# First inverse stage of a long convolution moved to two 64-row PE tiles, with a new order, engine choice and bank plan

## The chip, the cores and the metric

The kernel runs on one core of a Trainium2 chip. The metric is the device time of one execution in microseconds (us), lower is better. A core has five engines with queues of their own: TensorE (PE, matmuls into PSUM), VectorE (DVE), ScalarE (ACT), GpSimd (POOL) and SyncE (SP, which here issues nearly all DMAs). An engine works through its queue in order; semaphores make one engine wait for another.

## The reference, cut to what matters

Two layers, each a gated long convolution ("A") and an MLP ("B"), over 2048 tokens of 512 channels in bfloat16. Both layers use the same weights, and the convolution's inputs k and v do not depend on the layer, so its result y is needed only once.

```python
def _A_ref(q, k, v, shift_k, ssm_k, ssm_D):
    ...                                   # k_shift: causal 4-tap filter of k per channel
    kv = k_shift * v
    ...                                   # pad kv and ssm_k to 2*S, rfft2 of both
    y = irfft2(kv_f * kf_f)[:S]           # causal convolution of kv with ssm_k, per channel
    y = y + kv * ssm_D
    return q * y

def _B_ref(x, w1, b1, w2, b2):
    y = _layernorm(x)
    h = gelu(y @ w1 + b1)
    return h @ w2 + b2

x = A_q
x = x + _A_ref(_layernorm(x), A_k, A_v, A_shift_k, A_ssm_k, A_ssm_D)
x = x + _B_ref(_layernorm(x), B_w1, B_b1, B_w2, B_b2)
x = x + _A_ref(_layernorm(x), ...)        # the same y again
x = x + _B_ref(_layernorm(x), ...)
```

## The kernel before

**The convolution.** It is done by matmuls as a two-stage transform of 1024 points a half, the sequence being cut into two halves (tags end in _0 and _1). For the filter ("h") and for the product kv ("x") there is a first stage (`stage1`, L570, matmul L578: eight tiles of two PSUM banks, each of 16 matmuls) and a second (`stage2`, L583, matmul L590: eight tiles t of 16 matmuls). Every tile is then copied out of PSUM by ACT or DVE (`evac`, L477, with ACT at L480 and DVE at L481). The second stage reads a table of 16384 columns, R_S2. Its upper half is loaded by eight DMAs; its lower half (t below 4) is spread out on the chip from a compact table R_C of 1024 columns: eight operations, "spread" (L510 to L521), each multiply the compact table by a 0/1 mask of the partitions and write every eighth group of 16 columns. So the first second-stage tile with t below 4 needs all eight. They may go to ACT (L519) or DVE (L520). The filter is copied once more with its halves of the partitions exchanged, by DMAs called `swap` (L595).

Spectra are multiplied on DVE (L475, "products": for each of the eight tiles of x2_0 two of 128x1024, called g = 0 and g = 1). `inverse1` (L678, matmul L695) is the first inverse stage: eight tiles j of two banks. The tiles j = 0 to 3 read the products g = 0 of all eight x2_0 tiles, the tiles j = 4 to 7 the products g = 1. Its argument `split` chooses between two forms of the same sum: whole, 16 matmuls a tile with 128 rows of contraction and 128 columns; or split, 32 matmuls a tile, each with 64 rows of contraction and 64 columns, alternating between rows 0 to 63 (first bank) and rows 64 to 127 (second bank). The table R_U has zeros between the two halves of the rows, so both compute the same. Half 0 calls it whole (tag i1_0, L776), half 1 split (tag i1_1). `inverse2` (L705, matmul L717) is the second inverse stage: its matmuls read the results of all eight tiles of `inverse1`. Half 1 has the stages of its own (h2_1, p2, x1_1, x2_1, sum, i1_1, i2_1), which run while the MLP of half 0 does.

**The MLP.** Tokens go in blocks q0 to q12 of 128 to 512. For a block: statistics (bn_stats L831, L832), the reciprocal root on POOL (L836, L838), the normalisation on ACT or DVE (L856, L857), product with y and sum (L475), statistics again, normalisation, transposition (by PE for the first two token tiles, L908, else by DMA, L900), 11 tiles of the first matmul (m1, L920) with GELU on ACT (L925), and the second matmul (m2, L954) added on DVE (L958).

**The order.** The program is first written down as 1187 operations with a number each. Three literals then fix everything: SEQ is the order in which all operations are put on their engines' queues, ENGS names the engine (a, v, p) of each of the 233 operations that may go to more than one, BANKS gives the first PSUM bank of each of the 291 tiles. `arrange` (L214) applies them and adds the waits for PSUM banks; `sync` (L248) works out the semaphore waits. The numbers in `P.op(..., dur)` are the planner's costs; at run time they do nothing.

Of the kernel before, what the change touches and what calls it, by code (L numbers as in the profile page):

```python
# [36 lines left out]
class Prog:  # L37
# [62 lines left out]
    ENGS = (  # L100
            "pvavvvvvavpvpapapaaavaaaaavaavaavavvvppvvvaavvaaavaavvaaaaaaaaavaaaaavaaaavaaaaaaapppvaaaaaaaaaaaaaaaaaa"
            "avaaaaaaaaapvapvvavpvppaappvvpvaavpaappaappaappaappaappavppvappaappaappvappaapvaapvavvavvvvvapvvvvvppvaa"
            "avvvvaappavvapvavavpvvava")
    BANKS = (
# [294 lines left out]
def bass_interleave_layers__ssm_conv_h3__mixer_channel_mlp__prompt_kernel(  # L399
        nc, A_q, A_k, A_v, A_shift_k, A_ssm_k, A_ssm_D, B_x, B_w1, B_b1, B_w2, B_b2, out):  # L400
    P = Prog(nc)
# [101 lines left out]

    tload(t_s2, 18432, 0, R_C, 1024)
    load_h(0, R_1)
    load_t(A_k, 0, R_8, 2)
    load_t(A_v, 0, R_8 + 4096, 2)
    for i in range(8, 16):
        tload(t_s2, 18432, 2048 + i * 1024, R_S2 + i * 1024, 1024)
# [485 lines left out]
```

## Time and profile before

| what | value |
|---|---|
| time, median of 3 runs | 236.95 us (236.3 to 237.21) |
| span of the profiled execution, first to last instruction | 234.0 us |
| PE busy | 222.7 us, 95% of the span |
| DVE busy | 178.7 us, 76% |
| ACT busy | 164.5 us, 70% |
| POOL busy | 55.5 us, 24% |
| L695 whole (i1_0), 128 matmuls | 7.4 us busy |
| L695 split (i1_1), 256 matmuls | 5.0 us busy |
| granted TensorE clock | 1.000 |

The profiled execution's time is known by its span of 234.0 us; what lies around the span (launch and end) is the rest of an execution's time, 2.95 us by the median. In the rows quoted below, a row of the timeline gives start, duration, engine, line, operation, tiles and count, and in brackets the idle time before it; a row of the chain of waits gives start, duration and what the end of the program was waiting for then. A matmul's row ends when its last result lands, so a row is some 0.2 us longer than the time it keeps the next one back.

### The profile page before, as it was taken

The numbers are of one execution on the slowest core, as the hardware profiler recorded it, in microseconds if no ns is written. First come the engines' busy times: TensorE is split into PE (matmuls) and PEld (weight loads), VectorE is DVE, ScalarE is ACT, GpSimd is POOL, SyncE is SP. The second block draws the span as 40 slices with busy tenths as digits, with TensorE's granted clock in tenths as the row PEclk, the third lists the DMA queues.
The fourth block names the chain that finished last, engine by engine and source line by source line (L and its number), as shares of the span: only waits on it lengthen the run. The fifth ranks groups of instructions, "written<-read, shape, count | busy, mean of one in ns | idle before, by whom it ended". The sixth has DMA issues, their size and how long they took to land.

```text
span 234.0 us, 6498 instructions
## 1 busy us (share of the span) xinstructions
PE 222.7 (95%) x2743; PEld 147.1 (63%) x2765; DVE 178.7 (76%) x362; ACT 164.5 (70%) x262; POOL 55.5 (24%) x113
## 2 busy tenths in 40 slices
PE   7989887999999999999999999999999999999995
PEld 3878776967868596677966576644444444444454
DVE  0699998999999999999999988781777569410222
ACT  2789999989968688999879986488058216802710
POOL 2270132006403405639303331204011120200000
PEclk9999999999999999999999999999999999999999
DMA  6999489928994360033500313401300130170202
GB/s 185 381 386 305 147 229 274 324 65 150 144 211 126 70 158 3 1 48 72 155 4 3 90 24 68 134 3 22 69 0 3 28 62 0 23 115 0 90 0 92
DMA packets 40106, 24.93 MB, mean 107 GB/s; under 512 B 23591, under 2 KB 33677, under 8 KB 40077
## 3 DMA queue, kind: packets, MB, share of 16 engines
q1 hardware_dynamic: 39778, 24.36, 39.7%
q8 instruction: 22, 0.36, 0.7%
q10 hardware_dynamic: 298, 0.16, 0.4%
q14 instruction: 8, 0.06, 0.1%
HBM read 13.23 MB, written 2.10 MB: 66 GB/s over the span
## 4 chain that ended last, share of the span: by engine, by line
PE 58%; DVE 24%; ACT 10%; issue 2%; POOL 2%; DMA 2%; SPq 0%; DVEq 0%
PE ps L920 23%; PE ps L954 23%; DVE ar L475 13%; ACT ar L480 9%; PE ps L695 4%; DVE sm L831 3%; PE ps L590 2%; DMA ar<-in_A_ssm_k_dram 2%; DVE ar L672 2%; DVE ar L958 2%; DVE ar L641 2%; PE ps L717 1%; POOL sm L836 1%; PE ps L578 1%; PE ps L635 1%
## 5 line engine op out<-in xcount | busy, mean ns | idle before, releaser
L925 ACT ACTIVATE ar<-ps,sm 128x256 bf16<-128x256 f32 (+5 forms) x143 | 65.7, 523 | 33.2 <-PE ps L920 32.9
L920 PE MATMUL ps<-ar 128*128 128x256 bf16 (+5 forms) x569 | 81.9, 297 | 0.4 <-ACT ar L480 0.2
L480 ACT ACTIVATE ar<-ps 128x1024 bf16<-128x1024 f32 (+3 forms) x77 | 71.1, 998 | 11.0 <-PE ps L578 3.4
L954 PE MATMUL ps<-ar 128*128 128x512 bf16 (+1 forms) x323 | 75.9, 379 | 1.5 <-issue 0.6
L920 PEld LDWEIGHTS ps<-ar 128*128 128x128 bf16 (+1 forms) x572 | 52.9, 100 | 27.5 <-ACT ar L480 1.1
L475 DVE TENSOR_TENSOR ar<-ar 128x512 bf16<-128x512 bf16 (+2 forms) x104 | 62.7, 646 | 1.5 <-ACT ar L480 0.8
L954 PEld LDWEIGHTS ps<-ar 128*128 128x128 bf16 (+1 forms) x341 | 32.4, 98 | 35.3 <-ACT ar L925 0.4
L958 DVE TENSOR_TENSOR ar<-ar,ps 128x512 bf16<-128x512 bf16 x31 | 20.8, 680 | 32.9 <-PE ps L954 32.9
L831 DVE BATCH_NORM_STATS2 sm<-ar 128x6 f32<-128x512 bf16 x64 | 42.5, 685 | 0.5
L856 ACT ACTIVATE ar<-ar,sm 128x512 bf16<-128x512 bf16 x39 | 30.6, 813 | 12.9 <-DVE sm L843 8.8
L836 POOL TENSOR_SCALAR sm<-sm 128x2 f32<-128x2 f32 (+2 forms) x22 | 9.9, 449 | 89.0 <-DVE sm L832 88.8
L838 POOL TENSOR_TENSOR sm<-sm 128x2 f32<-128x2 f32 (+2 forms) x26 | 21.7, 834 | 25.1 <-DVE sm L836 23.1
L590 PE MATMUL ps<-ar 128*128 128x64 bf16 x512 | 18.4, 193 | 1.5 <-DVE ar L481 0.7
L578 PE MATMUL ps<-ar 128*64 128x128 bf16 x512 | 17.9, 221 | 1.8 <-ACT ar L480 1.2
L590 PEld LDWEIGHTS ps<-ar 128*128 128x128 bf16 x512 | 16.8, 98 | 3.6 <-DVE ar L481 1.3
L578 PEld LDWEIGHTS ps<-ar 128*64 128x64 bf16 x512 | 14.9, 110 | 4.8 <-ACT ar L480 1.9
L481 DVE CAST ar<-ps 128x1024 bf16<-128x1024 f32 x12 | 14.6, 1218 | 1.2 <-PE ps L578 0.9
L846 POOL TENSOR_SCALAR sm<-sm 128x1 f32<-128x1 f32 x34 | 15.1, 460 | 1.6
L695 PE MATMUL ps<-ar 64*128 64x64 bf16 (+1 forms) x384 | 12.4, 203 | 1.0 <-DVE ar L475 0.9
L695 PEld LDWEIGHTS ps<-ar 64*128 64x128 bf16 (+1 forms) x384 | 11.8, 113 | 2.2 <-DVE ar L475 1.0
L857 DVE TENSOR_SCALAR ar<-ar,sm 128x512 bf16<-128x512 bf16 x25 | 10.3, 415 | 2.7 <-POOL sm L846 2.5
L788 DVE SCALAR_TENSOR_TENSOR ar<-ar,sm,ps 128x512 bf16<-128x512 bf16 x16 | 11.1, 740 | 0.3 <-PE ps L590 0.3
(45 smaller groups left out, 93.5 us busy)
## 6 DMA issues: line engine op xcount, KB each, us to landing
ar<-ar SPq DMA_DIRECT2D x16, 256.0 KB, 4.0
ar<-tab_s SPq DMA_DIRECT2D x9, 256.0 KB, 6.3
ar<-in_A_ssm_k_dram SPq DMA_DIRECT2D x8, 256.0 KB, 5.9
ar<-in_A_q_dram SPq DMA_DIRECT2D x8, 256.0 KB, 4.4
ar<-in_A_v_dram SPq DMA_DIRECT2D x8, 256.0 KB, 5.0
out_dram<-ar SPq DMA_DIRECT2D x7, 256.0 KB, 2.5
ar<-in_B_w_dram SPq DMA_DIRECT2D x4, 344.0 KB, 5.2
ar<-in_B_w_dram SPq DMA_DIRECT2D x5, 256.0 KB, 5.2
```

What stands on the lines that cost most here:

```text
L475: return P.op(eng, lambda e: e.tensor_tensor(o, a, b, op), dur, reads=[a, b] + list(more), writes=[o])
L480: return e.activation(dst, src(), AF.Copy)
L578: r = e.matmul(Q(tl, 64 * ri, 64, i * 128, [1, 128]), w, m, start=True, stop=True)
L590: r = e.matmul(Q(tl, 0, 128, i // 8 * 512 + i % 8 * 4, [32, 16], [1, 4]), w, m, start=True, stop=True)
L695: r = e.matmul(Q(tl, 0, 128, i, *([32, 16], [1, 4]) if split else ([1, 128],)), w, m, start=n == 0, stop=n == 1)
L831: P.op(DVE, lambda e, sj=sj, x=x: e.bn_stats(sj, x), 600.0, reads=[x], writes=[sj])
L838: P.op(POOL, lambda e: e.tensor_tensor(r, v, hf, ALU.pow), 420.0 + 149.0 * n, reads=[v, hf], writes=[r])
L856: return e.activation(o, x, AF.Identity, bias=u, scale=r)
L920: r = e.matmul(Q(tl, 0, rows, 0, [1, w]), a, m, start=dk == 0, stop=dk == 3)
L925: P.op(ACT, lambda e, dst=dst, tl=tl, rows=rows, bias=bias, w=w: e.activation(dst, Q(tl, 0, rows, 0, [1, w]), AF.Gelu_apprx_tanh, bias=bia ...
L954: r = e.matmul(Q(tl, 0, 128, 0, [1, 512]), ins[fc][0], ins[fc][1], start=fc == 0, stop=fc == 10)
L958: P.op(DVE, lambda e, x=x, tl=tl: e.tensor_tensor(x, x, Q(tl, 0, 128, 0, [1, 512]), ALU.add), 604.0, reads=[x], writes=[x], tile=tl)
```

## The change

`inverse1` of half 0 is called with `split` on, the spread operations may go to POOL too, and SEQ, ENGS and BANKS are replaced whole. The other edits (a variable for the row length, a function for the eight transposing DMAs of half 1, a name for a lambda) give the same operations as before.

```diff
-    tload(t_s2, 18432, 0, R_C, 1024)
+    wide = 18432
+    for h in range(1):
+        tload(t_s2, wide, 1024 * h, R_C + 1024 * h, 1024)
...
-            P.op(BOTH, f, {ACT: 912.0, DVE: 395.0}, reads=[c, m], writes=[o])
+            P.op((ACT, DVE, POOL), f, {ACT: 1040.0, DVE: 395.0, POOL: 1050.0}, reads=[c, m], writes=[o])
...
     P.tag = "i1_0"
-    inverse1(R_1, R_2, R_3, False)
+    inverse1(R_1, R_2, R_3, 1)
...
-            "pvavvvvvavpvpapapaaavaaaaavaavaavavvvppvvvaavvaaavaavvaaaaaaaaavaaaaavaaaavaaaaaaapppvaaaaaaaaaaaaaaaaaa"
+            "vvpppppvavpvpvvvvaaavaaaaavaavaavavvavvppaaavvaaavvvvvaaaaaaaaaaaaaaavaaaavvaaaaaapppvaaaaaaaaaaaaaaaaaa"
...
```

Read against the list of operations, the literals say this. Of the eight spread operations (characters 2 to 9 of ENGS) before six were on DVE and two on ACT; now two are on DVE, one on ACT and five on POOL. All four transposed filter tiles of each half (ht0, ht1) are copied out by DVE (two of each were on ACT). DVE gives up one copy of x1_0, the one it had of x2_0 and one of the filter taps (fir3) to ACT, and takes a third one of i1_0. On POOL the five spread operations stand behind the reciprocal root of block q0 and the four tap products (L548); on PE the first second-stage tile (h2_0, t = 3) is number 25 of the queue (counted from 0), before it was number 26. On SP the first load of A_q is moved from tenth to fourth, ahead of A_k, the compact table and the last piece of the filter; the loads of R_S2, R_U and the weights change places, and the swap DMAs keep their places 35 to 43. In the queue of DVE two of ht1's copies stand among the products of x2_0, and two statistics of blocks q3 and q4 that stood behind the products stand before them. From the first matmul of the MLP on (PE number 75) the same operations follow, with one tile of m1 exchanged for another, in a new order.

More of the change, by code (lines that the diff above doesn't have):

```diff
@@ L44 @@
     SEQ = (
[55 rows of a table removed]
[55 rows of a table added]
     ENGS = (
-            "pvavvvvvavpvpapapaaavaaaaavaavaavavvvppvvvaavvaaavaavvaaaaaaaaavaaaaavaaaavaaaaaaapppvaaaaaaaaaaaaaaaaaa"
-            "avaaaaaaaaapvapvvavpvppaappvvpvaavpaappaappaappaappaappavppvappaappaappvappaapvaapvavvavvvvvapvvvvvppvaa"
-            "avvvvaappavvapvavavpvvava")
+            "vvpppppvavpvpvvvvaaavaaaaavaavaavavvavvppaaavvaaavvvvvaaaaaaaaaaaaaaavaaaavvaaaaaapppvaaaaaaaaaaaaaaaaaa"
+            "aaaaaaaaaaappappaavpvppaapvvvppaappaappaappaappaappaappvvppaapvaappaappvvppaappaapvvaavpvvvaavvvvaappvav"
+            "vppvavvvvvaaapvvaaavpvavv")
     BANKS = (
-            "26624320240260660466027405640260464422140204626240406006442460424046462022442640460444626002206020640220"
-            "04023022660051677767117660640311026376367637332542537030213654742352762454741476061377362300423726574027"
-            "07315704314621527766215047034261015330227471565340011503350731745320154030276054756")
+            "66434020640220260440227672640260464624760042000240002442422466624062460240442064660244626040204002640222"
+            "40064240717075704726312627456637417025016236523443374174025633103776205453260415317076222344700467503141"
+            "61262032456165157500527467025106024754623673201465073146475525064314245347541203406")
     def __init__(self, nc):
@@ L502, in load_t, with turn_k @@
             dma(A(0, 128, o + 512 * a, [1, 512 * w]), dr(x, 512 * (1024 * half + a), [8 * 512, 128], [1, 512 * w]), w << 17, paced=True)
-    tload(t_s2, 18432, 0, R_C, 1024)
+    wide = 18432
+    for h in range(1):
+        tload(t_s2, wide, 1024 * h, R_C + 1024 * h, 1024)
     load_h(0, R_1)
+    def turn_k(half):
+        for a in range(8):
+            src, dst = dr(A_k, 512 * (1024 * half + a), [8 * 512, 128], [1, 512]), A(0, 128, R_KT + 144 * a + 16, [1152, 4], [1, 128])
+            P.op(SP, lambda e, src=src, dst=dst: e.dma_start_transpose(dst, src), 1300.0, writes=[dst], dma=True, nbytes=1 << 17)
     load_t(A_k, 0, R_8, 2)
@@ L508, in bass_interleave_layers__ssm_conv_h3__mixer_channel_mlp__prompt_kernel @@
     for i in range(8, 16):
-        tload(t_s2, 18432, 2048 + i * 1024, R_S2 + i * 1024, 1024)
+        tload(t_s2, wide, 2048 + i * 1024, R_S2 + i * 1024, 1024)
     P.tag = "spread"
@@ L744, in bass_interleave_layers__ssm_conv_h3__mixer_channel_mlp__prompt_kernel @@
     turn(1, R_HRAW1, R_HP1)
+    lhs = lambda g: A(0, 128, R_HP1 + 64 * g, [1, 64])
     P.tag = "h1_1"
-    stage1(lambda g: A(0, 128, R_HP1 + 64 * g, [1, 64]), R_G1)
+    stage1(lhs, R_G1)
     P.tag = "x2_0"
@@ L797, in bass_interleave_layers__ssm_conv_h3__mixer_channel_mlp__prompt_kernel @@
     P.tag = "kt"
-    for a in range(8):
-        src, dst = dr(A_k, 512 * (1024 + a), [8 * 512, 128], [1, 512]), A(0, 128, R_KT + 144 * a + 16, [1152, 4], [1, 128])
-        P.op(SP, lambda e, src=src, dst=dst: e.dma_start_transpose(dst, src), 1300.0, writes=[dst], dma=True, nbytes=1 << 17)
+    turn_k(1)
     for c in (0, 2):
```

110 rows, old and new, of the table SEQ are left out of this document.

## The prediction

> **What bounds the kernel now.** I read the page first, then the windows, the chain of waits, and the timelines of single engines.
>
> ```profile
> span 234.0 us, 6498 instructions
> PE 222.7 (95%) x2743; PEld 147.1 (63%) x2765; DVE 178.7 (76%) x362; ACT 164.5 (70%) x262; POOL 55.5 (24%) x113
> ```
>
> By the page PE is the bound: 234.0 - 222.7 = 11.3 us idle. The windows (start:end, length, then busy time of PE, PEld, DVE, ACT, POOL) say where.
>
> ```profile
> 30.00:40.00 10.00, 8.46 (x248) 7.68 (x245) 9.18 (x14) 9.83 (x12) 2.92 (x8) 1.00 0.95 267
> 40.00:50.00 10.00, 8.81 (x167) 8.53 (x167) 9.70 (x18) 9.28 (x11) 0.10 (x1) 1.00 0.65 218
> 70.00:80.00 10.00, 9.79 (x200) 7.20 (x186) 10.00 (x24) 7.54 (x15) 3.19 (x8) 1.00 0.41 106
> ```
>
> Up to 50 us PE has the most idle time of the three stretches (1.54 and 1.19 us of 10) and ACT and DVE are nearly full. Later PE is full and DVE with it. The chain of waits shows the join, where i1_0 stands.
>
> ```profile
> 39.97 1.30 DVE ar L475 x2
> 41.27 0.05 issue
> 41.32 7.39 PE ps L695 x128
> 48.73 6.59 ACT ar L480 x8
> 55.33 0.05 issue
> 55.37 0.41 PE ps L908 x4
> 55.81 0.60 ACT ar L480
> 56.41 0.05 issue
> 56.46 0.84 PE ps L920 x12
> 161.16 6.49 PE ps L954 x30
> ```
>
> Products (DVE) release i1_0; its 128 matmuls stand whole on the path; then ACT's copies, the first transposition, and at 56.46 us the MLP begins. From there PE streams: 6.49 us for 30 matmuls is 216 ns each. So what the change is worth is how much earlier the MLP begins, as long as DVE, full from 70 us on, keeps up.
>
> **Part 1, i1_0 split.** PE's timeline has both forms, and the start of the next stage.
>
> ```profile
> 21.68 1.22 PE L590 MATMUL ps<-ar 128*128 128x64 bf16 x32
> 41.32 7.38 PE L695 MATMUL ps<-ar 128*128 128x128 bf16 x128 [0.90 <-DVE ar L475]
> 50.04 0.38 PE L717 MATMUL ps<-ar 128*128 128x512 bf16 x1 [0.33 <-ACT ar L480]
> 121.44 2.57 PE L695 MATMUL ps<-ar 64*128 64x64 bf16 x128
> 125.78 2.56 PE L695 MATMUL ps<-ar 64*128 64x64 bf16 x128
> ```
>
> Whole: 7.38 us for eight tiles, 0.92 a tile. Split: 2.57 + 2.56 = 5.13 us, 0.64 a tile, 20 ns a matmul. PE gives up 2.25 us. What hides part of it are the copies out of PSUM, whose number does not change, and the products. The Trainium skill ("TensorE: Matmul & The Clock Gate", Wait — 56ns, not 53.3ns?) has a floor of about 25 ns from one small matmul's start to the next; 256 of them would be an estimated 6.4 us and save 1.0 instead of 2.25. By it the last four tiles of Part 3 would end 0.6 us later and the sum would be 0.3 more. The row of 2.57 us for 128 lies below that floor, so the measurement decides; what the tiles would cost without running side by side is rival C.
>
> **Part 2, work moved in front of i1_0.** Steps come from successive starts, since rows overlap.
>
> ```profile
> 20.97 0.48 DVE L520 TENSOR_SCALAR ar<-ar,sm 128x1024 bf16<-128x1024 bf16 x1
> 21.36 1.22 DVE L481 CAST ar<-ps 128x1024 bf16<-128x1024 f32 x1
> 22.50 0.16 DVE L624 COPY ar<-ar 128x3 bf16<-128x3 bf16 x1
> 36.35 8.52 DVE L475 TENSOR_TENSOR ar<-ar 128x1024 bf16<-128x1024 bf16 x14 [0.82 <-ACT ar L480]
> 32.20 13.07 ACT L480 ACTIVATE ar<-ps 128x1024 bf16<-128x1024 f32 x14
> L481 DVE COPY ar<-ps 128x1024 bf16<-128x1024 bf16 x7 | 4.8, 683 | 7.6 <-PE ps L561 6.9 <-PE ps L610 0.7
> L519 ACT ACTIVATE ar<-ar,sm 128x1024 bf16<-128x1024 bf16 x2 | 2.3, 1164 | 0.0
> L857 DVE TENSOR_SCALAR ar<-ar,sm 128x512 bf16<-128x512 bf16 x25 | 10.3, 415 | 2.7 <-POOL sm L846 2.5
> 69.90 0.67 DVE ar L475 x2
> 70.57 1.20 DVE sm L831 x2
> ```
>
> A spread operation costs DVE 0.39 us (20.97 to 21.36), a float copy 1.14 (to 22.50), a bf16 copy about 0.6 (0.68 less the overlap), a product 0.61 (8.52/14), a statistic 0.60, a row product of 512 columns 0.33, a normalisation 0.41; ACT needs 0.93 a copy (13.07/14) and up to 1.16 for a spread operation.
>
> DVE, up to the last product g = 0 (which releases i1_0): out go four spreads (1.56), the fir3 copy (0.6), one copy each of x1_0 and x2_0 (2.28) and four small steps (0.3), 4.74 in all. In come four bf16 copies of ht0 and ht1 (2.4), the two statistics moved forward (1.2), two one-row additions (between 0.1 and 0.4 together, by 0.06 for a 128x3 copy and 0.42 a piece on POOL; I take 0.4) and four small steps (0.3): 4.3. Net -0.44.
>
> ACT, up to the last copy of x2_0: out go three bf16 copies, one h1_1 copy and one spread (4 x 0.93 + 1.16 = 4.9), in come three copies (2.8). Net -2.1.
>
> Both queues must arrive for i1_0. DVE binds with -0.44 plus whatever idle time goes: 0.82 us in the row at 36.35 alone, while it waited for an ACT copy that now comes up to 2.1 earlier. I take -1.2: i1_0 at 40.1. The ends are -0.2 (nothing but the load counts, and half of that is eaten by the load of A_q that now comes ahead of those of A_k) and -2.1 (ACT's whole relief).
>
> **Part 3, from there to the MLP.** On DVE six products g = 1 follow (6 x 0.61, to 43.75), then in its new queue three copies of i1_0, one normalisation and one small step (3.42 + 0.41 + 0.06): 47.6. On PE the last four tiles wait for those products and end at 43.75 + 4 x 0.64 = 46.3, the last copy on ACT at 47.3. So i2_0 starts at 47.7 against 50.04, 2.3 earlier, and now DVE is late, not PE. Of PE's 2.25 us only 1.1 is cashed here.
>
> Then ACT, from 47.3: a copy of h1_1 (0.93), two of i2_0 of half size (0.5 each), one of h1_1, two of i2_0 (0.93 each) to 52.0. Now it also has the normalisation z0, moved from DVE. Is that ready? On DVE two normalisations and the h1_1 copy come first (47.6 + 0.82 + 1.14), then two row products (0.66), a statistic (0.6) and two small steps: 51.1. On POOL stand these two steps:
>
> ```profile
> 53.31 0.33 POOL L836 TENSOR_SCALAR sm<-sm 128x1 f32<-128x1 f32 x1 [13.21 <-DVE sm L832]
> 53.72 0.63 POOL L838 TENSOR_TENSOR sm<-sm 128x1 f32<-128x1 f32 x1
> ```
>
> With a third like the first, POOL's 1.4 us bring it to 52.5. ACT: z0 0.8 (53.3), one i2_0 copy (54.25), the copy of the transposed tile 0.6: MLP at 54.9 against 56.46, **-1.55**. From there PE's work is the same, streamed; DVE's load up to the end of the products of half 1 is net 1.1 us smaller (5.64 out, 4.55 in, by the steps above) and its earlier start adds to that, so it keeps up.
>
> **Part 4, the spread on POOL.** Its one-input price is not in the trace. The nearest rows:
>
> ```profile
> L872 POOL MEMSET ar<- 1x512 bf16 x2 | 1.0, 519 | 9.7 <-PE ps L695 9.7
> L872 POOL MEMSET ar<- 1x256 bf16 x2 | 0.6, 306 | 0.1
> L548 POOL TENSOR_TENSOR ar<-ar 128x256 bf16<-128x256 bf16 x4 | 2.4, 612 | 3.3 <-DVE ar L481 3.1
> L475 POOL TENSOR_TENSOR ar<-ar 1x128 bf16<-1x128 bf16 x4 | 1.7, 420 | 3.6 <-ACT ar L480 2.9 <-DVE ar L481 0.8
> 12.22 1.99 POOL L548 TENSOR_TENSOR ar<-ar 128x256 bf16<-128x256 bf16 x3 [3.07 <-DVE ar L481]
> ```
>
> No input: 0.83 ns a column (519 - 306 over 256), 0.95 us for 1024. Two inputs: 1.5 ns a column (612 - 420 over 128), 1.76 us; scaled flatly from 612, 2.45. I take 1.2, between the slopes and nearer the first. POOL's queue reaches the first spread after q0's root and the last tap product. Before, the tap products began at 12.22, held by the copy of the taps from PSUM. That copy is now fourth in DVE's queue and two of the products stand ahead of q0's root, so I put the first spread where the first of them stood, at 12.4; five end at 12.4 + 5 x 1.3 = 18.9. The first second-stage tile should run at 21.68 - 1.2 = 20.5. So up to 1.6 us a piece is hidden; the cover is POOL's empty time.
>
> **Sum.** Span 234.0 - 1.55 = 232.4; with the 2.95 us that the median has over the span, 235.4. PE's own small gaps after 56 us (0.21 of the window 70 to 80) are reshuffled by the new order, either way. **Forecast 235.4 us.**
>
> **Rivals.**
>
> A, *slower*: POOL is held while DVE reads two tensors from SBUF. The trace has it:
>
> ```profile
> 90.16 3.48 DVE L475 TENSOR_TENSOR ar<-ar 128x2048 bf16<-128x2048 bf16 x3
> 90.35 3.35 POOL sm L836
> ```
>
> A POOL step of some 0.3 us lasted 3.35 while DVE multiplied without a pause. If spreads are held to 2.45 us each, five end at 12.4 + 5 x 2.55 = 25.1; the first second-stage tile, and all of PE's in-order queue behind it, runs 3.4 us later than now and i1_0 with it; Part 3's remaining -0.35 stays: 236.95 + 3.4 - 0.35 = 240.0. It decides from 1.6 us a piece. Against it: between 12 and 19 us DVE's queue holds copies from PSUM, statistics and fir products with one SBUF input, hardly any two-input step. The Trainium skill ("SBUF — State Buffer", Who interferes with whom) says that only DVE steps with two SBUF inputs, or in two-port modes, hold a POOL step that reads SBUF; by that rule A stays away. Chance 0.11.
>
> B, *no change*: DVE and the loads set the pace. The front keeps only -0.2, the rest as in Part 3: -0.55, 236.4; or DVE, full at 70 us, passes on less than PE gained. For it: DVE's 10.00 of 10. Chance 0.23.
>
> C, *the tiles do not run side by side* in i1_0, so the change of form does nothing. Then a matmul costs what a 64-column one on the full array does:
>
> ```profile
> 65.27 0.95 PE ps L590 x32
> ```
>
> 30 ns, 256 of them 7.6 us, no less than 7.38; the last four tiles end at 47.5, a copy at 48.5 against DVE's 47.6: -1.55 + 0.9 = -0.65, 236.3. The rows of i1_1 speak against it: 0.02.
>
> D, *more*: the front gives ACT's 2.1 and i1_0 ends as early again: -2.45 to -3.4, about 234.0. Chance 0.13.
>
> **How the numbers follow.** Forecast 0.51, A 0.11, B 0.23, C 0.02, D 0.13. What a measurement can tell from no change is 0.5%, 1.18 us: faster is below 235.77. The forecast's own spread, 234.5 to 236.2, lies mostly there: 0.43 of its 0.51, with D 0.56. Of A 0.10 and of B 0.04 are slower: 0.14. The rest, 0.30, is the same. The range 233.5 to 237.6 leaves out nearly all of A and a little of D.
>
> **What would show it.** L695 in 64x64 form 512 times, i1_0 near 40 us and 5.1 to 6.5 us long with DVE, not PE, ending it; L520 on POOL near 1.2 us; h2_0 before 21 us; the first L920 near 54.9. Wrong if POOL's spread row is over 1.6 us with PE's L590 waiting for it, if the first L920 is not earlier than 56, or if PE gains gaps over 1 us in all behind it.

## The result, and the profile after

The changed kernel takes 246.43 us (median of 4, 245.93 to 247.83), the kernel before 236.62 us beside it (4 runs, 235.6 to 237.21): ratio 1.044, 95% interval 1.0397 to 1.0483, slower by 9.8 us. The ratios here and below leave out executions over 1.5% above the shortest of their kernel and are not quotients of the medians shown, from which they differ by up to 0.3%. Forecast were 235.4 us, range 233.5 to 237.6. The profiled execution took 245.93 us with a span of 244.0, 10.0 us more than before. Line numbers are 5 or 6 higher than before (the spread is L526, the first-stage matmul L584, the second-stage one L596, i1_0 L701, m1 L925); in the experiments they shift again, and the text names the work.

Lines of the page of after:

```profile
span 244.0 us, 6782 instructions
PE 223.9 (92%) x2893; PEld 145.3 (60%) x2893; DVE 177.2 (73%) x358; ACT 164.1 (67%) x261; POOL 67.4 (28%) x121
...
PE   7893498689899999899999998999999999999996
...
PEclk9999599999999999999999999999999999999999
...
q8 instruction: 23, 0.38, 0.6%
...
L596 PE MATMUL ps<-ar 128*128 128x64 bf16 x512 | 20.0, 196 | 8.5 <-POOL ar L526 7.0
...
L526 POOL TENSOR_SCALAR ar<-ar,sm 128x1024 bf16<-128x1024 bf16 x5 | 14.2, 2847 | 0.5
```

and the row of the second stage on the page before:

```profile
L590 PE MATMUL ps<-ar 128*128 128x64 bf16 x512 | 18.4, 193 | 1.5 <-DVE ar L481 0.7
```

PE does nearly the same work (223.9 against 222.7 us busy) in a longer span, so nearly all of the 10 us is idle time. One group names most of it: 7.0 us ahead of the second stage, ended by a spread on POOL, each 2.85 us long. The hole shows in the PE slices as "34", and in the second of these two slices the clock is at half.

The timeline of after, first POOL:

```profile
12.60 2.86 POOL L526 TENSOR_SCALAR ar<-ar,sm 128x1024 bf16<-128x1024 bf16 x1
...
15.72 11.66 POOL L526 TENSOR_SCALAR ar<-ar,sm 128x1024 bf16<-128x1024 bf16 x4
```

then DVE:

```profile
21.89 0.18 DVE L837 BATCH_NORM_AGGREGATE sm<-sm 128x2 f32<-128x6 f32 x1
30.43 1.22 DVE L481 CAST ar<-ps 128x1024 bf16<-128x1024 f32 x1 [8.36 <-PE ps L584]
```

and PE:

```profile
27.53 1.01 PE L596 MATMUL ps<-ar 128*128 128x64 bf16 x16 [7.00 <-POOL ar L526]
...
48.44 1.25 PE L701 MATMUL ps<-ar 64*128 64x64 bf16 x64 [1.11 <-ACT ar L480]
...
56.05 1.04 PE L723 MATMUL ps<-ar 128*128 128x512 bf16 x4
...
63.10 0.87 PE L925 MATMUL ps<-ar 128*96 128x128 bf16 x12
...
103.94 1.08 PE L584 MATMUL ps<-ar 128*64 128x128 bf16 x32 [1.24 <-ACT ar L480]
```

The fifth spread ends at 27.38 us, and the first second-stage tile, 21.68 before, runs at 27.53. The granted clock was 0.50 for 6.83 us, in the hole and behind it (24.78 to 31.61): 16 such matmuls take 1.01 us there and 0.64 at full clock. The first MLP matmul comes at 63.10 instead of 56.46, 6.64 later. From it to the end the span has 244.0 - 63.10 = 180.9 us, before 234.0 - 56.46 = 177.5: another 3.4 us. Two terms, then: **6.6 up to the MLP, 3.4 behind it**. The waits of PE behind 54 us show the second one, before and after:

```profile
PE ps L954 <- issue: 0.6, 4, 0.2
PE ps L908 <- ACT ar L480: 0.3, 1, 0.3
...
```

```profile
PE ps L925 <- ACT ar L930: 1.6, 3, 1.0
PE ps L584 <- ACT ar L480: 1.2, 1, 1.2
PE ps L913 <- ACT ar L861: 0.4, 1, 0.4
...
```

(Total us, times, longest.) The longest wait of before was 0.3 us; now PE stops 1.0 us for a GELU and 1.2 us for a copy out of PSUM. In all these waits are 3.8 us against 1.3, so they hold 2.5 of the 3.4.

### The profile page after: what moved, and what is told of

It is laid out like the page before. It is cut to its first block, busy times and chain, and to the rows that moved or that the text cites. A ratio compares the mean times of both kernels' runs of the same rounds, so it can differ in the third digit from the quotient of the medians.

```text
span 244.0 us, 6782 instructions
## 1 busy us (share of the span) xinstructions
PE 223.9 (92%) x2893; PEld 145.3 (60%) x2893; DVE 177.2 (73%) x358; ACT 164.1 (67%) x261; POOL 67.4 (28%) x121
## 4 chain that ended last, share of the span: by engine, by line
PE 52%; DVE 25%; POOL 11%; ACT 5%; DMA 4%; issue 2%; SPq 0%; DVEq 0%; POOLq 0%
PE ps L959 24%; PE ps L925 21%; DVE ar L475 11%; POOL ar L526 6%; DVE sm L836 5%; DVE ar L481 4%; DMA ar<-ar 3%; PE ps L596 2%; POOL sm L843 2%; ACT ar L930 2%; PE ps L584 2%; DMA ar<-in_A_ssm_k_dram 2%; POOL sm L851 2%; ACT ar L861 2%; DVE ar L963 1%
## 5 line engine op out<-in xcount | busy, mean ns | idle before, releaser
L925 PE MATMUL ps<-ar 128*128 128x256 bf16 (+5 forms) x572 | 82.5, 297 | 1.8 <-ACT ar L930 1.6
L959 PE MATMUL ps<-ar 128*128 128x512 bf16 (+1 forms) x341 | 79.0, 379 | 0.4 <-ACT ar L861 0.4
L925 PEld LDWEIGHTS ps<-ar 128*128 128x128 bf16 (+1 forms) x572 | 52.6, 100 | 29.9 <-ACT ar L930 3.0
L475 DVE TENSOR_TENSOR ar<-ar 128x512 bf16<-128x512 bf16 (+3 forms) x106 | 62.7, 632 | 2.6 <-DMA ar<-ar 1.1
L841 POOL TENSOR_SCALAR sm<-sm 128x2 f32<-128x2 f32 (+2 forms) x22 | 6.7, 305 | 101.1 <-DVE sm L837 100.1
L843 POOL TENSOR_TENSOR sm<-sm 128x2 f32<-128x2 f32 (+2 forms) x26 | 23.3, 896 | 21.8 <-DVE sm L841 19.9
L596 PE MATMUL ps<-ar 128*128 128x64 bf16 x512 | 20.0, 196 | 8.5 <-POOL ar L526 7.0
L596 PEld LDWEIGHTS ps<-ar 128*128 128x128 bf16 x512 | 17.7, 100 | 11.3 <-issue 7.3
L584 PE MATMUL ps<-ar 128*64 128x128 bf16 x512 | 18.9, 228 | 1.9 <-ACT ar L480 1.8
L584 PEld LDWEIGHTS ps<-ar 128*64 128x64 bf16 x512 | 15.8, 114 | 4.5 <-ACT ar L480 2.7
L481 DVE CAST ar<-ps 128x1024 bf16<-128x1024 f32 x10 | 12.0, 1211 | 8.8 <-PE ps L584 8.8
L526 POOL TENSOR_SCALAR ar<-ar,sm 128x1024 bf16<-128x1024 bf16 x5 | 14.2, 2847 | 0.5
L701 PE MATMUL ps<-ar 64*128 64x64 bf16 x512 | 10.0, 195 | 2.0 <-ACT ar L480 1.1
L701 PEld LDWEIGHTS ps<-ar 64*128 64x128 bf16 x512 | 9.3, 114 | 3.6 <-ACT ar L480 1.9
```

Of the source, the lines that this page charges most:

```text
L475: return P.op(eng, lambda e: e.tensor_tensor(o, a, b, op), dur, reads=[a, b] + list(more), writes=[o])
L526: return e.tensor_scalar(o, c, m, None, ALU.mult)
L584: r = e.matmul(Q(tl, 64 * ri, 64, i * 128, [1, 128]), w, m, start=True, stop=True)
L596: r = e.matmul(Q(tl, 0, 128, i // 8 * 512 + i % 8 * 4, [32, 16], [1, 4]), w, m, start=True, stop=True)
L843: P.op(POOL, lambda e: e.tensor_tensor(r, v, hf, ALU.pow), 420.0 + 149.0 * n, reads=[v, hf], writes=[r])
L925: r = e.matmul(Q(tl, 0, rows, 0, [1, w]), a, m, start=dk == 0, stop=dk == 3)
```

## The experiments

My theory: the loss is the price of a spread on POOL plus waits in the new order. Rivals: DVE holds POOL (rival A of the prediction); the split itself loses; the half clock is the loss.

**What a spread costs on POOL.** The kernel before, with two rounds of six POOL operations of 1024 columns behind everything else (in short; o_scattered is the spread's own output, o_flat a contiguous one):

```diff
+    e.tensor_scalar(o_scattered, c, m, None, ALU.mult)
+    e.tensor_scalar(o_flat, c, m, None, ALU.mult)
+    e.tensor_scalar(o_flat, c, 2.0, None, ALU.mult)
+    e.tensor_copy(o_flat, c); e.tensor_tensor(o_flat, c, c2, ALU.mult); e.memset(o_flat, 0.0)
```

> The kernel before with twelve extra GpSimd operations at the end of its queue, where it is idle; they write to the spent second-stage table. Two rounds of six on 1024 columns: the spread as it is (mask per partition, 64 runs of 16 columns 128 apart), the same with a contiguous output, a constant factor contiguous, a contiguous copy, a product of two tensors, a memset. If the scattered output makes the price, the first takes 2.85 us and the second to fourth about 1.0 to 1.3; if the operation itself does, the first two or three take 2.85 and the copy about 1.0 to 1.3; if VectorE held the spreads in the changed kernel, all are well below 2.85 here, where VectorE is nearly idle. The product of two should take 1.8 (slope of the rows) to 2.45 us, the memset 0.95 to 1.05.

The timeline of POOL in this kernel, in the order of the diff:

```profile
201.25 2.85 POOL L969 TENSOR_SCALAR ar<-ar,sm 128x1024 bf16<-128x1024 bf16 x1
204.20 2.84 POOL L970 TENSOR_SCALAR ar<-ar,sm 128x1024 bf16<-128x1024 bf16 x1
207.13 2.77 POOL L971 TENSOR_SCALAR ar<-ar 128x1024 bf16<-128x1024 bf16 x1
209.97 1.04 POOL L972 COPY ar<-ar 128x1024 bf16<-128x1024 bf16 x1
211.09 2.12 POOL L973 TENSOR_TENSOR ar<-ar 128x1024 bf16<-128x1024 bf16 x1
213.27 0.96 POOL L974 MEMSET ar<- 128x1024 bf16 x1
```

The scattered write costs nothing (2.85 and 2.84), the mask next to nothing (2.77 with a constant). It is the operation: a multiplication by a scalar, 2.7 ns a column, is dearer on POOL than a product of two tensors (2.12 us), and a copy costs a third (1.04). The Trainium skill ("GPSIMD Engine Reference", 4.1 Engine selection) calls POOL "roughly line-rate" with one input; here that may fit the copy (1.0 ns a column) but not the scalar multiplication, which takes DVE 0.39 us.

Rival A falls with the rows of after: from 22.07 to 30.43 us DVE had nothing to do, and the spreads ran on at 2.85 us each, as the first did while DVE worked. By the Trainium skill ("SBUF — State Buffer", Who interferes with whom) a DVE step with at most one SBUF input, outside the two-port modes, does not hold POOL; the trace agrees as far as it goes, since no spread was longer while DVE worked.

**The same kernel with a cheap spread.** After, with the five POOL spreads as plain copies. It leaves out the mask in those five.

```diff
+                if e is nc.gpsimd:
+                    return e.tensor_copy(o, c)
                 return e.tensor_scalar(o, c, m, None, ALU.mult)
```

> The changed kernel in which the five GpSimd operations copy the compact table without multiplying by the mask (this leaves the mask out of those five). A contiguous copy of 1024 columns took 1.04 us in the probe, so the five end at 12.6 + 5 x 1.15 = 18.4 us or a little more if the scattered output costs. Theory, the price of 2.85 us was the one wrong size of the prediction and the rest stands: 234.5 to 236.2 us. Rival, the new order and the split lose by themselves: about 239 us, as with the spreads back on VectorE and ScalarE.

238.31 us (10 runs, 236.3 to 240.62), ratio 1.0081 (1.0053 to 1.011). PE's timeline:

```profile
39.72 1.26 PE L703 MATMUL ps<-ar 64*128 64x64 bf16 x64 [0.71 <-ACT ar L480]
...
45.35 1.22 PE L703 MATMUL ps<-ar 64*128 64x64 bf16 x62 [0.64 <-issue]
...
47.69 1.04 PE L725 MATMUL ps<-ar 128*128 128x512 bf16 x4
...
54.73 0.87 PE L927 MATMUL ps<-ar 128*96 128x128 bf16 x12
```

With 1.04 us a piece the front comes out as predicted (i1_0 40.1, i2_0 47.7, first m1 54.9), and 8.1 of after's 9.8 us are gone. But the MLP starts 1.73 us earlier than before and the span, 235.9, is 1.9 longer: 235.9 - 54.73 = 181.2 us behind the start, as in after.

**The spreads back on DVE and ACT.** After, with the eight letters of before in ENGS.

```diff
-            "vvpppppvavpvpvvvv...
+            "vvavvvvvavpvpvvvv...
```

> The changed kernel with its eight spread operations on the engines that they had before (six on VectorE, two on ScalarE), all else as changed. Theory 1, the five GpSimd spreads of 2.85 us each make the whole loss by holding the first second-stage tile (27.53 against 21.68 us) and letting the clock fall: that tile comes back to 21 to 22 us, the granted clock is 1.000, and the time is 234.5 to 237.5 us. Theory 2, the new order loses by itself as well (the stretch from the MLP's start to the end was 3.4 us longer than before: 10.0 in all less 6.6 at the first matmul of the MLP): the time stays at 239 to 241 us with matmul gaps of 3 us or more behind 60 us.

239.12 us (4 runs, 238.61 to 240.62), ratio 1.0131 (1.0089 to 1.0173): the POOL price is worth 7.3 us, and the new order loses without it too. In its profile (of the longest of the four) the MLP starts at 57.74 us, later than before, and 238.7 - 57.74 = 181.0 us stand behind it, as in after. So the front gains nothing here. The swap DMAs may be a part of that: in SP's queue they stand two places further back than before, not in the same places as said above, and in the kernel with two spreads on POOL (below) DVE waits 1.78 us for such a transfer just ahead of the products. In the same kernel with i1_0 whole again (`split` off):

> The changed kernel with the spread operations on the engines of before and i1_0 whole again: only the new order, engines and banks are left of the change. If the order alone loses, 238 to 240.5 us, with the stop of about 2.5 us for ScalarE near 96 us and the products waiting for the swap transfers near 40 us, as in the run with the spreads back. If what was lost there came from the split form, 235.5 to 237 us.

241.02 us (4 runs, 240.34 to 242.82), ratio 1.0202 (1.0159 to 1.0245). The new order with its engines and banks, without split and POOL spreads, loses 4.7 us between the medians. The split seems to gain 1.9 of them, but the two intervals overlap a little, so how much is not sure.

**Two spreads on POOL.** After, with three of the five back on DVE.

> The changed kernel with two spread operations on GpSimd instead of five, the other three on VectorE. Theory 1: two of 2.85 us from 12.6 end at about 18.6, ahead of the first second-stage tile at 20.5 to 21.5, so they cost nothing: the time is that of the run with none on GpSimd within 1 us. If any use of GpSimd there costs time (by holding VectorE, or by delaying the roots of the first blocks), it lies between that run and the changed kernel in proportion, 2 to 4 us above.

The four executions took 239.39, 243.13, 244.8 and 245.3 us, too far apart for a median; the first is like the kernel with none on POOL (239.12). The profile is of the last. From POOL's timeline and then PE's:

```profile
16.35 2.84 POOL L526 TENSOR_SCALAR ar<-ar,sm 128x1024 bf16<-128x1024 bf16 x1
```

```profile
23.26 0.64 PE L596 MATMUL ps<-ar 128*128 128x64 bf16 x16 [1.50 <-DVE ar L526]
```

The second spread on POOL ends at 19.19 us, and the first second-stage tile waits for one on DVE: in this execution two are hidden. Its length comes from behind: PE stops 2.50 us at 63.4 us ("issue": it waited for nothing that the profile shows), and the clock is at half for 3.41 us twice, with none on POOL once. Why the stop of 2.50 us comes stays open.

**The old order behind the new front.** The first 297 of the 1187 operations, up to the first transposition for the MLP, stand as in after, all others in the order, on the engines and in the banks of before (the diff in short); once with the copies (mask left out, as above), once with the spreads as after has them.

```diff
-    SEQ = after
+    SEQ = after[:297] + [i for i in before if i not in after[:297]]
```

> The kernel of f6_copy_price (five spreads on POOL as unmasked copies, so the mask is left out of those five) up to its first MLP transposes, and from there the order, the engines and the banks of the kernel before. Theory: what f6 lost behind the start of the MLP (54.73 us to the end 181.2 us, against 177.5 us before) is the new order's own waits there (0.51, 0.99 and 1.33 us of PE at 67.8, 83.9 and 95.8 us). With the old order behind it, the first MLP matmul stays at 54.7 us, the rest takes 177.5 us again, the span is 232.3 us and the time some 234.4 us, ratio 0.992. Rival: whatever order stands behind it, a stage that starts 1.7 us earlier waits for transfers, DVE and ACT, which do not come earlier; then the span is 234.0 us or more and the ratio 1.00 to 1.01.

235.72 us (12 runs, 234.64 to 236.63), ratio 0.9971 (0.9954 to 0.9989).

> The kernel after, its five spreads as it has them, up to its first MLP transposes, and from there the order, the engines and the banks of the kernel before. Theory: the loss of after is two terms that add: 6.6 us up to the first MLP matmul (63.10 against 56.46 us) from the spreads on POOL, and 3.4 us behind it from the new order's waits. With the old order behind it the first MLP matmul stays at 63.1 us and the rest takes 177.5 us again as it did with the copies: span 240.6 to 241.5 us, time 242.5 to 243.5 us, ratio 1.026 to 1.030. Rival: the two are not independent, transfers and DVE's work that the new order put off pile up behind a late front whatever the order: ratio 1.04 or more.

243.94 us (5 runs, 243.55 to 244.52), ratio 1.0323 (1.0302 to 1.0343). The first m1 matmul, with the copies:

```profile
55.36 0.84 PE L922 MATMUL ps<-ar 128*128 128x128 bf16 x12 [0.69 <-ACT ar L475]
```

and with the spreads as in after:

```profile
64.72 0.84 PE L920 MATMUL ps<-ar 128*128 128x128 bf16 x12 [0.69 <-ACT ar L475]
```

The spans are 232.9 and 242.3, so what stands behind the start takes 177.5 and 177.6 us: with the old order always the same, whether the MLP starts at 55.4, 56.5 or 64.7 us. With the new order it took 180.9 (after) and 181.2 (with copies). The 3.4 us belong to the new order with its engines and banks, which were exchanged together, and not to the late front, and the rival of both expectations, that an earlier or later front changes what follows, falls. The join costs 0.6 us (55.36 against 54.73) and 1.6 in the second kernel, where i1_0 also has two stops marked "issue" of 0.52 and 0.91 us (after has one of 0.28; the next experiments treat them); hence 1.032 and not 1.030.

Where those 3.4 us are lost can be read, though I isolated no single one. The timeline of the kernel with copies, all engines:

```profile
91.50 1.01 ACT L480 ACTIVATE ar<-ps 128x1024 bf16<-128x1024 f32 x1
91.79 2.21 POOL L853 TENSOR_SCALAR sm<-sm 128x1 f32<-128x1 f32 x4
...
94.03 0.81 ACT L863 ACTIVATE ar<-ar,sm 128x512 bf16<-128x512 bf16 x1 [1.52 <-POOL sm L853]
94.75 1.92 ACT L480 ACTIVATE ar<-ps 128x1024 bf16<-128x1024 f32 x2
...
95.81 1.08 PE L586 MATMUL ps<-ar 128*64 128x128 bf16 x32 [1.33 <-ACT ar L480]
```

ACT's queue has a normalisation (L863) ahead of two copies of x1_1. It waits 1.52 us for the root on POOL. The copies behind it wait too, though the data of the first are there, and PE waits for that first one, which ends at 95.7. In the timeline of the kernel before, five of x1_1's eight copies stand ahead of the normalisation, which hardly waits:

```profile
94.59 1.02 ACT L480 ACTIVATE ar<-ps 128x1024 bf16<-128x1024 f32 x1
95.77 0.81 ACT L856 ACTIVATE ar<-ar,sm 128x512 bf16<-128x512 bf16 x1 [0.16 <-POOL sm L846]
```

**The split alone.** The kernel before with `split` on.

```diff
-    inverse1(R_1, R_2, R_3, False)
+    inverse1(R_1, R_2, R_3, True)
```

> The kernel before with i1_0 split and nothing else: order, engines and banks as before. If the split form runs side by side in i1_0 as in i1_1, i1_0 needs 5.1 us or somewhat more and the MLP begins 0.5 to 2.2 us earlier: 234.5 to 236.1 us. If the copies out of PSUM are what sets that stage, or the split form buys nothing, 236.3 to 237.0 us.

237.79 us (7 runs, 236.48 to 239.62), ratio 1.0052 (1.0023 to 1.0082): less work on PE, and no gain. The profile is of the longest of the seven (239.62 us); in three of the others the clock stayed at 1.000. In it i1_0 lasts from 41.95 to 51.04 us, longer than the 7.38 of the whole form. PE's timeline in i1_0:

```profile
47.29 0.25 PE L695 MATMUL ps<-ar 64*128 64x64 bf16 x3 [0.48 <-DVE ar L481]
49.20 1.84 PE L695 MATMUL ps<-ar 64*128 64x64 bf16 x61 [1.66 <-issue]
```

A stop of 1.66 us in the middle of a tile, with nothing to wait for ("issue"), while the DMA engines were full of MLP weights up to 47 us (share 0.95 from 41 to 47); in it the half clock begins, for 6.83 us. The page's instruction queue (q8: 23 transfers, 0.38 MB, 16 KB each; before 22, and the split adds 128 pairs of weight load and matmul) suggested a block of PE's own instructions. If so, the stop stands at a fixed place in PE's stream. Next: the warm-up ahead of everything as 30 matmuls of 128 columns instead of 7 of 512, which is 23 instruction pairs more.

```diff
-        for i in range(7):
-            r = e.matmul(Q(tl, 0, 128, 0, [1, 512]), z[:, :128], z, ...)
+        for i in range(30):
+            r = e.matmul(Q(tl, 0, 128, 0, [1, 128]), z[:, :128], z[:, :128], ...)
     inverse1(R_1, R_2, R_3, True)
```

> The kernel before with i1_0 split, as in the run of the split alone, and the seven warm-up matmuls of 512 columns replaced by thirty of 128 columns (about the same time, 23 weight-load and matmul pairs more ahead of everything). With the split alone TensorE stopped for 1.66 us after the third matmul of the seventh tile of i1_0, inside a run that waits for nothing. Theory, the stop is at a fixed instruction of TensorE's stream, where the next 16 KB block of instructions (queue q8) had not come: it moves 23 pairs earlier, to about the twelfth matmul of the sixth tile, or is gone where the block comes in time. Rival, it belongs to that tile (its bank, a wait, a transfer of data): it stays at the seventh tile. Time 236.5 to 239 us if there is still a stop and half clock behind it, 234.5 to 235.5 without.

238.77 us (10 runs, 236.97 to 241.08), ratio 1.0079 (1.0048 to 1.0111). PE's timeline:

```profile
45.32 1.21 PE L695 MATMUL ps<-ar 64*128 64x64 bf16 x44 [0.29 <-DVE ar L475]
47.83 1.58 PE L695 MATMUL ps<-ar 64*128 64x64 bf16 x84 [1.30 <-issue]
```

The stop moved by 23 pairs: these last four tiles now break after 44 matmuls, before after 64 + 3 = 67. So it sits at an instruction, not at a time or at data. Counted in PE's stream, 982 matmuls are ahead of it in both, and 981 ahead of the stops in the same stage of after and of the kernel with copies. In three kernels (this, the split alone, the one with copies) one 16 KB transfer of the instruction queue had ended 1.3 to 1.5 us before PE went on. The Trainium skill ("Runtime: NRT & Kernel Launch", Instruction fetch mechanics) has each engine's instructions streamed in blocks of 16 KiB, 256 instructions, and the cost "mostly hidden"; the stop shows a case where it isn't. By that figure a block holds 128 pairs, which PE uses up in an estimated 2.6 us at 20 ns a matmul and in 7.4 in the whole form.

To see whether the weights delay the block, all nine weight loads were held until the fifth tile of i1_0:

```diff
+        late = [o for o in self.seq if 201 <= o.i <= 209]
...
+        late[0].preds[226] = "raw"
     inverse1(R_1, R_2, R_3, True)
```

> The kernel before with i1_0 split, and the nine loads of the MLP's weights held back until i1_0's last tile (2.7 MB that in the run of the split alone were under way at 38 to 47 us, with the DMA engines full). Theory, the instruction block was late because it stood behind those loads: the stop of 1.66 us goes, the clock stays at 1.000, i1_0 lasts 5.2 to 7 us, and the time is 234.0 to 235.8 us unless the weights then come too late for the first MLP matmul (about 55 us). Rival, the split form cannot be fed at 20 ns a matmul for 256 in a row however free the queues are: the stop stays, 236.5 to 238.5 us.

238.8 us (9 runs, 236.38 to 239.08), ratio 1.0079 (1.0049 to 1.0109). The stop is gone, and the price is paid at the MLP:

```profile
58.16 1.43 PE L925 MATMUL ps<-ar 128*128 128x128 bf16 x12 [2.32 <-DMA ar<-in_B_w_dram]
```

Last, only three of the seven early loads (201, 207, 203), held until the last tile of i1_0:

> The kernel before with i1_0 split, and three of the seven early MLP weight loads held until the last matmul of i1_0 is done. Theory: the stop in i1_0 is a block of PE's instructions that comes late behind those loads; with three fewer in the way it is gone or under 0.5 us, i2_0 starts near 49.4 us as where all nine were held (ACT's copies, 0.9 us each, set that time, not PE), and no MLP matmul waits over 0.5 us for a weight, as the three have over 6 us to land. Time 0.3 to 0.8 us under that of the kernel before, ratio 0.997 to 0.999. Rival: the block comes late with or without the loads, or the three come late in their turn: a stop of 1 us or more is left at one of the two places and the ratio is 1.004 or more.

235.69 us (12 runs, 234.73 to 236.96), ratio 0.9969 (0.995 to 0.9987). No stop, no late weight; this version computes everything and beats both kernels, by little. Why so little, ACT's and PE's rows say. ACT's timeline before:

```profile
30.37 17.65 ACT L480 ACTIVATE ar<-ps 128x1024 bf16<-128x1024 f32 x19 [0.17 <-PE ps L590]
48.73 6.59 ACT L480 ACTIVATE ar<-ps 128x1024 bf16<-128x1024 f32 x8 [0.71 <-PE ps L695]
```

and in this kernel, then PE's:

```profile
31.18 24.02 ACT L485 ACTIVATE ar<-ps 128x1024 bf16<-128x1024 f32 x27 [0.17 <-PE ps L595]
```

```profile
49.93 0.38 PE L722 MATMUL ps<-ar 128*128 128x512 bf16 x1 [0.33 <-ACT ar L485]
...
56.35 0.84 PE L925 MATMUL ps<-ar 128*128 128x128 bf16 x12 [0.22 <-ACT ar L485]
```

ACT copies tiles out of PSUM without a pause for 24 us; before it had one pause, of 0.71 us, for i1_0's matmuls. From the start of that stretch to the first MLP matmul it is 26.09 us before (30.37 to 56.46) and 25.17 here (31.18 to 56.35), so PE's 2.25 us come to 0.9: the copies take PE's place as the bound. The profiled spans (234.0 and 233.9) hide that, since the stretch began 0.8 later in this execution; the kernel before with the probe behind it has 30.88, so that start varies between executions. Between the medians the gain is 0.7 us.

**The clock.** After, with 30 matmuls of 512 columns, whose results nobody reads, ahead of the first second-stage tile.

```diff
+        for i in range(30):
+            r = e.matmul(Q(tl, 0, 128, 0, [1, 512]), IDN, z, start=True, stop=True)
```

> The kernel after with 30 matmuls of 512 columns, whose results nobody reads, ahead of the first second-stage tile on PE, so that PE works (30 times 0.213 us, 6.4 us) while POOL spreads. Theory: the spreads hold i1_0 and the half clock (6.83 us in the profile of after, 24.78 to 31.61 us) is only what follows from PE's idle time; its price is at most the 4.1 us that PE worked at half clock, halved, 2 us, and since PE waits for POOL, DVE and ACT in that stretch much of it is hidden: first second-stage tile still at 27.4 us or later, i1_0 at 47 to 48.4 us, time 0 to 2 us under 246.4 us. Rival: the half clock is most of the loss up to i1_0 (7.1 us): then i1_0 starts at 44 us or earlier and the time is 243 us or less.

246.96 us (4 runs, 246.63 to 247.8), ratio 1.0456 (1.043 to 1.0483): no better than after. PE's timeline:

```profile
20.10 6.64 PE L975 MATMUL ps<-ar 128*128 128x512 bf16 x30
27.54 0.63 PE L596 MATMUL ps<-ar 128*128 128x64 bf16 x16 [0.81 <-POOL ar L526]
...
46.63 1.26 PE L701 MATMUL ps<-ar 64*128 64x64 bf16 x64 [1.02 <-ACT ar L480]
...
61.70 0.87 PE L925 MATMUL ps<-ar 128*96 128x128 bf16 x12
...
103.44 1.39 PE L584 MATMUL ps<-ar 128*64 128x128 bf16 x32 [2.70 <-ACT ar L480]
```

The clock held at 1.00 through the front, i1_0 came 1.8 us earlier and the MLP 1.4. Both were given back at the copy of x1_1, where PE now stops for 2.70 us instead of 1.24, and in a half-clock window of 3.41 us behind that stop. The half clock follows from the hole: it is at most 1.4 of the 6.6 us up to the MLP, and without it the time is no shorter.

## Why the prediction was wrong, step by step

- **Part 4, the price of a spread: wrong, and the main fault.** Taken 1.2 us, bounds 0.95 to 2.45; measured 2.85, above both ends. I bounded a one-input multiplication by a memset and a two-input product, as if the number of inputs set the price; the probe shows 2.84 for the one-input multiplication against 2.12 for the product. The rest of the step held: the first spread at 12.60 (12.4 forecast), and pieces of 1.04 us, under the 1.6 that were to be covered, left no wait. Five pieces end at 27.38 instead of 18.9.
- **Part 1, the split: right on PE** (64 matmuls in 1.25 us, 20 ns each). It had no term for the instruction stream, which stops PE for 0.28 us in after, 0.64 with the copies and 1.66 with the split alone. Undone, it makes the new order some 1.9 us slower, by intervals that overlap a little.
- **Part 2, the front, and Part 3 up to the MLP: right, given the price.** With copies i1_0 starts at 39.72 (40.1), i2_0 at 47.69 (47.7), m1 at 54.73 (54.9). Some of that is luck: i1_0 was released there by a copy on ACT (0.71 us) and not by DVE's products, which were to bind.
- **Part 3, "from there PE's work is the same, streamed": wrong.** PE's work is the same, but the new order (with its engines and banks) has stops in it, 180.9 us instead of 177.5. I argued from DVE's load, which was indeed no larger (177.2 against 178.7 us busy), and did not read the order in ACT's queue, where a normalisation that waits for POOL holds up copies that PE needs.
- **The sum:** 6.6 (price) + 3.4 (order) = 10.0 of span. With both faults mended (copies, old order) the span is 232.9 against the forecast 232.4; but that execution is the second shortest of twelve, and between the medians the gain is 0.6 us (235.72 against 236.35) of the forecast 1.55. The 2.95 us around the span were too much: 1.8 to 1.9 lie there in every run (234.71 - 232.9), since the median of before had been set against one of its shorter executions.
- **Rival A** had the side and the point from which it decides (1.6 us a piece), with 240.0, but not the reason: POOL wasn't held, the operation is that slow. Its price of 2.45 was still too low. **B** and **D** assumed a hidden spread; **C** is refuted by the 20 ns.
- **What would show it:** "POOL's spread row is over 1.6 us with PE's L590 waiting for it", "the first L920 is not earlier than 56" and "PE gains gaps over 1 us in all behind it" were the three signs named as wrong. All came (2.85 us a piece, 63.10, 2.5 us of waits more).

## What to carry to other kernels

An operation moved to an engine on which the trace doesn't show it has no bound from other operations there, however alike they look: measure that one operation at its size before anything is built on it. When an order is replaced whole, read for each in-order queue what stands behind every operation that waits for a third engine; here the new order behind the MLP's start cost 3.4 us, twice what the front had won with a cheap spread (1.7), and an ACT normalisation ahead of two copies made one of its stops, of 1.2 to 1.3 us. And a stage cut short on one engine gains only up to the next queue that feeds or empties it, here ACT's copies and PE's own instruction stream.

## What the runs showed of the hardware

- POOL, 1024 columns of bf16: scalar multiplication 2.77 to 2.85 us, two-input product 2.12, copy 1.04, memset 0.96.
- PE can run short of instructions: among short matmuls (20 ns) and under full DMA queues it stopped 1.3 to 1.7 us at a fixed instruction, and fewer loads at that time removed the stop. Full queues aren't all of it: with the spreads as in after and the old order behind, PE stopped 0.91 us in the same stage while the DMA share was 0.03.
- In or behind stops of PE of 1.66 to 7.06 us the granted clock fell to 0.50 for 3.41, 6.83 or 10.24 us; behind others, of 1.30 to 2.50 us, it stayed at 1.00. In this kernel a filled hole kept the clock at 1.00 up to the MLP and left the time as it was (246.96 against 246.43 us).
